# A placing model whose two DMA rings share the engines by packet size, and two kinds of work offered some microseconds later

## The chip, the cores and the metric

The kernel runs on one core of one Trainium2 chip. TensorE (PE in the profile) multiplies, ScalarE (ACT) evaluates functions and copies, VectorE (DVE) does element-wise work, GpSimd (POOL) and SyncE (SP) issue transfers here. The metric is device microseconds, the median of several executions; lower is better. The kernel before takes 735.46 us (three runs, 735.04 to 735.61).

## The reference, cut to what matters

```
x : 2048 x 640 (f32);  32 heads of 20
A: qkv = x @ wqkv;  pq, pk = phi(q), phi(k)      phi(t) = (t + 1 if t > 0 else exp(t)) + 1e-6
   kv = sum_s pk^T v;  z = sum_s pk
   o = (pq @ kv) / (pq . z + 1e-6)               per head and row
   a = o @ wo
B: h = sigmoid(x @ w_gate) * (x @ w_up)          640 -> 1536
   b = h @ w_down                                1536 -> 640
g = sigmoid(sum(x * gate_w))
result = g * a + (1 - g) * b
```

## The kernel before, in words

Every f32 matmul is done as three passes over values that are split into a high and a low half (`mm3`, lines 404 to 406). `split` (line 434) makes the halves: ScalarE writes the high half, VectorE then the low one. Sums of blocks of x, of weights and of hidden values save block products, so VectorE and ScalarE have a lot to add and split beside the matmuls.

The program has these stages:

- Stage 1 makes k from x and gathers x^T phi(k), from which kv follows later.
- Stage 2 (`q_phase` and `f_phase` with `pr` = 1) does the second 1024 rows of x. It makes q, the matrix M (kv times wo, for all heads together), and the twelve hidden blocks f = 0 to 11 of B. Each block's weights are loaded raw (`wst`), split and summed (`queue_g`, `queue_s`), and the finished halves and sums are stored in DRAM (`wf`). The pieces are called `wg`, `wu` and `ws`; a block's seven products `s1` to `s7` fill the PSUM tiles `ch`, `dd` and `cc`, and ScalarE copies some of them out into tiles `c` and `cx` before PE goes on adding in the same bank.
- Stage 3 does the same for the first 1024 rows. The finished weights are loaded from DRAM. After each second hidden block a pair of blocks goes through w_down (`down_pair`, line 1838); its weights are one tile `wf`, loaded in three parts by `load_wf` (line 1630): columns 640 to 1280 first, then 0 to 640, then the sums.
- Stage 4 multiplies the scaled phi(q) by M and finishes the output.

Two side works run in stage 3, beside the hidden blocks:

- Denominators (`queue_dens`, line 1399), for two groups of 512 rows at a time. POOL loads phi(q) tiles (`pden`), VectorE adds them up weighted into `fac`. The sums go to DRAM (`den_dram`) and come back turned (`turn_in`); `factor` adds the turned parts, takes the reciprocal and multiplies by the gate. The result is stored (`fac_dram`) and comes back turned once more (`turn_out`).
- M's rows (`queue_m`, line 1675), five row groups u = 0 to 4, one after the other in one tile. SP loads the rows in four transfers (`mr<-m_dram`), ScalarE and VectorE split them (`mt<-mr`), POOL stores the split rows (`mp_dram<-mt`), and the next group's load follows the split.

The order of the instructions on each engine is decided when the program is built, by the class `Order`. It keeps a clock for PE, ACT and DVE, with costs of `a_cost` and `v_cost`. Work is queued with a function that tells when its inputs are there (`ready`); `fill` gives an item its place when its inputs are there by these clocks and it ends soon enough behind PE (`_fits`). Transfers have a clock too: `Ring` stands for one of two queues, SP's and POOL's, and `Rings.issue` works out when a transfer lands if both queues have transfers under way. The builder's clocks set only the order; on the chip, engines wait for semaphores, in that order.

The lines that the change touches: `Rings.issue` (308), `Ring.dma_start` (352), `turn_in` (1420) and `queue_m` (1675). The result of `Rings.issue` is read by every `order.when(...)`, so that a changed landing time can move any queued work.

Of the kernel before, what the change touches and what calls it, by code (L numbers as in the profile page):

```python
# [15 lines left out]
S, D, F = 2048, 640, 1536  # L16
H, DH = 32, 20
KC = D // P
# [284 lines left out]
class Rings:  # L303
# [1 line left out]
    def __init__(self):  # L305
        self.q = [[], []]

    def issue(self, n, arrive, took):
        cell = [0.0]
        self.q[n].append((arrive, took, cell))  # L310
        i, t, left = [0, 0], 0.0, [None, None]
        q = self.q
        while True:
            for k in range(2):
                if left[k] is None and i[k] < len(q[k]) and q[k][i[k]][0] <= t:
                    left[k] = q[k][i[k]][1]
            live = [k for k in range(2) if left[k] is not None]
            coming = [q[k][i[k]][0] for k in range(2) if left[k] is None and i[k] < len(q[k])]
            if not live:
                if not coming:  # L320
                    break
                t = min(coming)
                continue
            dt = min([left[k] * len(live) for k in live] + [c - t for c in coming])
            t += dt
            for k in live:
                left[k] -= dt / len(live)
                if left[k] <= 1e-9:
                    q[k][i[k]][2][0] = t + 0.5
                    left[k] = None  # L330
                    i[k] += 1
        return cell


class Ring:

    def __init__(self, engine, order, rings, n, issue, lag):
        self.engine, self.order, self.rings, self.n, self.issue, self.lag = engine, order, rings, n, issue, lag
        self.t = 0.0
# [12 lines left out]
    def dma_start(self, out, src, **kw):  # L352
        o = self.order
        start = max(self.t, o.data(out, [src]))
        self.t = start + self.issue
        (r1, n), (r2, _) = (self.run(ap, 0 if getattr(ap.tensor, "_space", DRAM) == DRAM else 1) for ap in (out, src))
        r = min(r1, r2)
        took = 1.25 * max(1, n // r) * (7 + 0.0377 * r) / 16e3
        self.cell = self.rings.issue(self.n, start + self.lag, took)
        o.put(out, [src], self.cell)  # L360
        return self.engine.dma_start(out, src, **kw)

# [2 lines left out]
def a_cost(w):  # L365
    return 0.06 + w / 1200

def v_cost(w):
    return 0.07 + w / 960

@with_exitstack
def gated_mix_kernel(ctx: ExitStack, tc: tile.TileContext, xt, xn, wk, wv, wo, wst_q, wst_f, out_t):
# [6 lines left out]
    order = Order()  # L379
# [3 lines left out]
    def f32(ap):  # L383
        return ap.bitcast(F32)
# [34 lines left out]
    def vec2(out, a, b, op, after=""):  # L419
        order.on_vec(width(out), after, 1.0, out, a, b)  # L420
        nc.vector.tensor_tensor(out, a, b, op=op)  # L421

    def vec3(out, a, scalar, b, op0, op1, after=""):
        order.on_vec(width(out), after, 1.0, out, a, b)
        nc.vector.scalar_tensor_tensor(out, a, scalar, b, op0=op0, op1=op1)

    def vec1(out, a, s0, s1=None, op0=OP.mult, op1=None, after=""):
        order.on_vec(width(out), after, 1.0, out, a)
        if op1 is None:
            nc.vector.tensor_scalar(out, a, s0, None, op0=op0)  # L430
        else:
            nc.vector.tensor_scalar(out, a, s0, s1, op0=op0, op1=op1)

    def split(hi, lo, src, after=""):
        act(hi, src, AF.Copy, after)
        at = order.act + A_LAG

        def low():
            order.vec = max(order.vec, at)
            vec2(lo, src, f32(hi), OP.subtract)  # L440
        order.then(low)

    def add(out, a, b, after=""):
        vec2(out, a, b, OP.add, after)

    def sub(out, a, b, after=""):
        vec2(out, a, b, OP.subtract, after)
# [7 lines left out]
    fac = common.tile([P, NG, TG], F32, name="fac")  # L455
# [77 lines left out]
    class Chunk:  # L533
# [39 lines left out]
        def sum(self, n):  # L573
            x = self.x
            b11, b12, b21, b22 = x[0][:, 0:2], x[1][:, 0:2], x[0][:, 2:4], x[1][:, 2:4]
            self.T = (b11, b22, b12, b21)
            if n == 0:
                sub(b11, b12, b11)
            elif n == 1:
                sub(b12, b22, b12)  # L580
            elif n == 2:
                sub(b22, b22, b11)
            else:
                sub(b21, b21, b22)
# [434 lines left out]
    g = GTBatch(0, [0])  # L1019
# [8 lines left out]
    for c in range(1, 4):  # L1028
        ck = chunks[c]
        if c == 1:  # L1030
# [14 lines left out]
            g = GTBatch(c, batches[c])  # L1045
# [97 lines left out]
        if c > 1:  # L1143
            g = GTBatch(c, batches[c])
# [50 lines left out]
    def tt(name, dt=F32, shape=(P, TG)):  # L1195
        return pw.tile(list(shape), dt, name=name, tag="t", bufs=4)
# [202 lines left out]
    def queue_dens(*gs2):  # L1399

        st = {}

        def load(g, u):
            if u < KC:
                st[g, u] = tt("pden")
                gp.dma_start(st[g, u], p_dram[:, u, g])
                st["at", g, u] = lambda: order.when(st[g, u])

        def one(g, u):
            td = fac[:, g]  # L1410
            if u == 0:
                vec1(td, st[g, u], zcol[:, 0:1], zeps[:, 0:1], OP.mult, OP.add)
            else:
                vec3(td, st[g, u], zcol[:, u:u + 1], td, OP.mult, OP.add)
            load(g, u + 2)
            if u == KC - 1:
                gp.dma_start(den_dram[:, g], td)
                st["at", g, u + 1] = lambda: order.when(den_dram[:, g])

        def turn_in(g):  # L1420
            for j in range(4):
                js = slice(j * H, (j + 1) * H)
                gp.dma_start(fac[js, g].rearrange("h (d c) -> h d c", c=P),
                                  den_dram[:, g, j * P:(j + 1) * P].rearrange("(d h) c -> h d c", h=H))
            st[g, "gs"] = tt("gs")[:, :P]
            sp.dma_start(st[g, "gs"], gate_rep[4 * g:4 * g + 4].rearrange("i h c -> (i h) c"))
            st["at", g, KC + 1] = lambda: max(order.when(fac[:, g]), order.when(st[g, "gs"]))

        def factor(g):
            td = fac[:, g]  # L1430
            q = td[:, :P]
            add(td[:, :2 * P], td[:, :2 * P], td[:, 2 * P:])
            add(q, q, td[:, P:2 * P])
            order.on_vec(5 * P, "")
            nc.vector.reciprocal(q, q)
            vec2(q, q, st[g, "gs"], OP.mult)
            gp.dma_start(fac_dram[:, g], q)
            st["at", g, KC + 2] = lambda: order.when(fac_dram[:, g])

        def turn_out(g):  # L1440
            for d in range(4):
                sp.dma_start(fac[d * H:(d + 1) * H, g].rearrange("h (j c) -> h j c", c=P),
                                  fac_dram[:, g].rearrange("(j h) c -> h j c", h=H))
        order.add(0, 0, lambda: [load(g, u) for u in range(2) for g in gs2], chain=True)
        for u in range(KC):
            for g in gs2:
                order.add(0, v_cost(TG), lambda g=g, u=u: one(g, u), None, lambda g=g, u=u: st["at", g, u](), chain=True)
        for n, (v, fn) in enumerate(((0, turn_in), (2.0, factor), (0, turn_out))):
            for g in gs2:
                order.add(0, v, lambda g=g, fn=fn: fn(g), ("fac", g) if n == 2 else None,  # L1450
                          lambda g=g, n=n: st["at", g, KC + n](), chain=True)
# [217 lines left out]
    def m_rows(dst, cols, queue, u=None):  # L1669

        for d in range(4):
            m = m_dram.rearrange("(h u d) n -> d h u n", u=KC, d=4)[d]
            queue.dma_start(dst[d * H:(d + 1) * H], m[:, u] if cols is None else m[:, :, cols])

    def queue_m(u=0):

        raw = down_pool[1].tile([P, D], F32, name="mr", tag="mr")
        m_rows(raw, None, sp, u)

        def fn():  # L1680
            t = down_pool[1].tile([P, 2, D], F32R, name="mt", tag="mt")
            split(t[:, 0], t[:, 1], raw)

            def rest():
                gp.dma_start(mp_dram[:, u], f32(t))
                if u + 1 < KC:
                    queue_m(u + 1)
            order.then(rest)
        order.add(a_cost(D), v_cost(D), fn, "m", lambda: order.when(raw), spare=True)

    def m_close():
        nonlocal tb
# [510 lines left out]
    q = q_phase(1, lambda k: [(b12h[:, k], b12l[:, k])], extra)  # L2203
# [33 lines left out]
    q = q_phase(0, lambda k: [(c_h[c][:, k], c_l[c][:, k]) for c in range(2)], {})  # L2237
# [383 lines left out]
```

## Time and profile before

| | |
|---|---|
| median of 3 runs | 735.46 us (735.04 to 735.61) |
| the profiled execution | 735.37 us; its span 733.6 us |
| PE busy | 727.4 us, 99% of the span |
| DVE, ACT, POOL busy | 561.5, 358.6, 114.0 us |
| DMA | 173.54 MB, mean 237 GB/s |
| granted TensorE clock | 1.00 |

The profile lists, for one execution, the instructions of each engine with start and duration, what each waited for, and the transfers. Times within it count from the start of the span. `x4` at the end of a timeline row means four instructions merged in one row; the bracket names the idle time of the engine just before, and what ended it. In stage 3 the hidden blocks run from about 440 us on.

### The profile page before, as it was taken

The page shows a single profiled execution, that of the slowest core. Times are in us where ns is not written, and L with a number is a line of the kernel's source. Part 1 is how long each engine was busy: PE and PEld are TensorE (multiplying, and loading weights), DVE is VectorE, ACT ScalarE, POOL GpSimd, SP SyncE. Part 2 cuts the span into 40 slices and gives each one's busy share as a digit, 9 for nine tenths or more (in the row PEclk, how much of TensorE's full clock was granted, in tenths as well). Part 3 has the DMA queues.
Part 4 walks back from the last instruction along what each step waited for, and adds up shares of the span by engine and source line. Part 5 has one row for each costly group of instructions (what it writes and reads, how often), then busy time and mean ns, then how long its engine had stood idle before and what let it go on. Part 6 is the DMA issues. An engine that isn't in the chain of part 4 may idle for free.

```text
span 733.6 us, 10128 instructions
## 1 busy us (share of the span) xinstructions
PE 727.4 (99%) x3575; PEld 623.3 (85%) x3575; DVE 561.5 (77%) x987; ACT 358.6 (49%) x668; POOL 114.0 (16%) x197
## 2 busy tenths in 40 slices
PE   9999999999999999999999999999999999999998
PEld 8999999988788888888888888888787888888886
DVE  4978787987677989898989973466766775688783
ACT  5765648358556653535355363454333232324550
POOL 0211111113211211111210033023011331000000
PEclk9999999999999999999999999999999999999999
DMA  8464648697877866457687289878968597759212
GB/s 270 119 189 120 186 108 250 151 334 284 295 271 264 327 240 242 183 215 257 256 326 265 102 291 373 321 240 280 363 242 326 172 324 204 273 207 347 76 69 101
DMA packets 68873, 173.54 MB, mean 237 GB/s; under 512 B 11690, under 2 KB 31418, under 8 KB 65238
## 3 DMA queue, kind: packets, MB, share of 16 engines
q1 hardware_dynamic: 50342, 103.70, 42.7%
q0 software_dynamic: 18336, 69.03, 26.7%
q8 instruction: 28, 0.46, 0.3%
q14 instruction: 23, 0.19, 0.1%
q10 hardware_dynamic: 144, 0.16, 0.1%
HBM read 103.96 MB, written 63.92 MB: 229 GB/s over the span
## 4 chain that ended last, share of the span: by engine, by line
PE 86%; DMA 6%; issue 4%; DVE 2%; ACT 1%; POOL 1%; SPq 0%; POOLq 0%; ACTq 0%; DVEq 0%
PE ch L404 9%; PE ch L406 9%; PE ch L405 9%; PE cc L404 7%; PE cc L405 7%; PE cc L406 7%; PE dd L404 7%; PE dd L406 7%; PE dd L405 7%; PE rot L404 6%; PE rot L406 5%; PE rot L405 5%; DMA mr<-m_dram 2%; DMA pden<-p_dram 2%; DMA wg<-wf 1%
## 5 line engine op out<-in xcount | busy, mean ns | idle before, releaser
L417 ACT ACTIVATE c<-ch 128x512 f32<-128x512 f32 x52 | 31.1, 598 | 91.4 <-PE ch L406 91.3
L421 DVE TENSOR_TENSOR hf<-c,hf 128x512 fp32r<-128x512 f32 x75 | 51.2, 688 | 21.1 <-ACT hf L417 20.7
L417 ACT ACTIVATE hf<-c 128x512 fp32r<-128x512 f32 x75 | 46.1, 624 | 26.0 <-DVE c L421 26.0
L421 DVE TENSOR_TENSOR c<-cc,c 128x512 f32<-128x512 f32 x40 | 27.6, 689 | 40.6 <-PE cc L406 29.2
L404 PE MATMUL ch<-xth,ws 128*128 128x512 f32 x112 | 43.8, 391 | 0.0
L406 PE MATMUL ch<-xth,ws 128*128 128x512 f32 x112 | 43.6, 389 | 0.0
L405 PE MATMUL ch<-xtl,ws 128*128 128x512 f32 x112 | 43.6, 389 | 0.0
L421 DVE TENSOR_TENSOR tb<-rot,tb 128x512 f32<-128x512 f32 (+1 forms) x61 | 39.5, 677 | 3.0 <-PE rot L406 3.0
L421 DVE TENSOR_TENSOR tb<-dd,tb 128x512 f32<-128x512 f32 x44 | 30.3, 688 | 9.4 <-PE dd L406 9.4
L404 PE MATMUL dd<-xrh,wg 128*128 128x512 f32 x90 | 35.2, 391 | 0.0
L406 PE MATMUL dd<-xrh,wg 128*128 128x512 f32 x90 | 35.1, 389 | 0.0
L405 PE MATMUL dd<-xrl,wg 128*128 128x512 f32 x90 | 35.0, 389 | 0.0
L417 ACT ACTIVATE c<-dd 128x512 f32<-128x512 f32 x22 | 13.1, 598 | 41.4 <-PE dd L406 41.4
L404 PE MATMUL cc<-xbh,ws 128*128 128x512 f32 x84 | 32.7, 389 | 0.0
L405 PE MATMUL cc<-xbl,ws 128*128 128x512 f32 x84 | 32.7, 389 | 0.0
L406 PE MATMUL cc<-xbh,ws 128*128 128x512 f32 x84 | 32.7, 389 | 0.0
L421 DVE TENSOR_TENSOR c<-c,c 128x512 f32<-128x512 f32 x46 | 31.6, 688 | 1.3 <-ACT c L417 0.7
L417 ACT ACTIVATE dd<-ch 128x512 f32<-128x512 f32 x22 | 12.8, 582 | 35.0 <-PE ch L406 35.0
L421 DVE TENSOR_TENSOR wst<-wst 128x256 f32<-128x256 f32 (+2 forms) x69 | 27.4, 413 | 1.5
L404 PE MATMUL rot<-pkh,xnh 128*128 128x320 f32 x90 | 28.1, 312 | 0.1
L405 PE MATMUL rot<-pkl,xnh 128*128 128x320 f32 x90 | 27.8, 309 | 0.0
L406 PE MATMUL rot<-pkh,xnl 128*128 128x320 f32 x90 | 27.8, 309 | 0.0
(650 smaller groups left out, 2350.8 us busy)
## 6 DMA issues: line engine op xcount, KB each, us to landing
wf<-ws POOLq DMA_DIRECT2D x12, 1152.0 KB, 7.7
ws<-wf SPq DMA_DIRECT2D x11, 1152.0 KB, 9.5
wst<-wst_f SPq DMA_DIRECT2D x12, 640.0 KB, 5.2
wf<-wg POOLq DMA_DIRECT2D x12, 640.0 KB, 6.4
wd<-wd POOLq DMA_DIRECT2D x12, 640.0 KB, 8.0
wg<-wf SPq DMA_DIRECT2D x12, 640.0 KB, 5.8
wf<-wd SPq DMA_DIRECT2D x10, 640.0 KB, 10.1
xnst<-xn SPq DMA_DIRECT2D x16, 320.0 KB, 4.3
```

What stands on the lines that cost most here:

```text
L404: nc.tensor.matmul(out, l_hi, r_hi, start=first, stop=False, skip_group_check=True)
L405: nc.tensor.matmul(out, l_hi, r_lo, start=False, stop=False, skip_group_check=True)
L406: nc.tensor.matmul(out, l_lo, r_hi, start=False, stop=last, skip_group_check=True)
L417: nc.scalar.activation(out, src, fn, **kw)
L421: nc.vector.tensor_tensor(out, a, b, op=op)
```

## The change

In the builder's model, two transfers under way on both queues shared the 16 DMA engines half and half. Now each has a share in proportion to 7 + 0.0377 times its packet length in bytes, the length cut at 2600. And two kinds of work are offered later than the model's landing: the adding of the turned denominators by 4 us, the split of M's rows by 3 us. No instruction computes anything else than before.

```diff
-    def issue(self, n, arrive, took):
+    def issue(self, n, arrive, took, share):
         cell = [0.0]
-        self.q[n].append((arrive, took, cell))
+        self.q[n].append((arrive, took, cell, share))
...
-            dt = min([left[k] * len(live) for k in live] + [c - t for c in coming])
+            all_ = sum(q[k][i[k]][3] for k in live)
+            part = {k: q[k][i[k]][3] / all_ for k in live}
+            dt = min([left[k] / part[k] for k in live] + [c - t for c in coming])
             t += dt
             for k in live:
-                left[k] -= dt / len(live)
+                left[k] -= dt * part[k]
...
-        self.cell = self.rings.issue(self.n, start + self.lag, took)
+        self.cell = self.rings.issue(self.n, start + self.lag, took, 7 + 0.0377 * min(r, 2600))
...
-            st["at", g, KC + 1] = lambda: max(order.when(fac[:, g]), order.when(st[g, "gs"]))
+            st["at", g, KC + 1] = lambda: max(order.when(fac[:, g]), order.when(st[g, "gs"])) + 4
...
-        order.add(a_cost(D), v_cost(D), fn, "m", lambda: order.when(raw), spare=True)
+        order.add(a_cost(D), v_cost(D), fn, "m", lambda: order.when(raw) + 3, spare=True)
```

What this does to the built program, engine by engine (the two orders laid side by side):

- PE has the same matmuls in the same order.
- ACT and DVE differ at three places. At two places in stage 2, raw weights are split later: one split of 640 columns (`wg<-wst`) goes behind a copy `c<-ch`; and in hidden block f = 0 the split `wg` of the next block's weights goes from ahead of the loading of a function table to behind the copy `c<-ch` that follows it. The sums of that block's weights (`wst<-wst`) and its split `ws` come later with it: on ACT the copy `cx<-ch` now stands ahead of the split `ws`, and on DVE the addition `cx<-cc,cx` stands between the second and the third of the five sums.
- At the third place, in stage 3, the five splits of M's rows each move back by some instructions, and the factors of the first two groups of denominators, side by side before, are now apart: the first behind the split of row group 2, the second behind the split `hf` of the next hidden block.
- SP issues the rows of groups 2 and 3 later: before, groups 0, 1 and 2, then `gs`, `wu`, `wg`, `ws`, three parts of `wf`, group 3, `wu`; now groups 0 and 1, `gs`, `wu`, group 2, `wg`, `ws`, three parts of `wf`, `wu`, group 3. Group 4 stays behind `fac<-fac_dram`.
- POOL stores row group 0 behind `den_dram<-fac` instead of ahead of it, and group 1 behind `fac<-den_dram` instead of ahead of it. The stores of groups 2 to 4 keep their places, and `pden<-p_dram` of the next two groups stays behind the store of group 4.

## The prediction

> **What bounds the kernel now.** First the page, for the engines' shares:
>
> ```profile
> span 733.6 us, 10128 instructions
> PE 727.4 (99%) x3575; PEld 623.3 (85%) x3575; DVE 561.5 (77%) x987; ACT 358.6 (49%) x668; POOL 114.0 (16%) x197
> ```
>
> PE is the bound, and its matmuls stay the same. So the change can only win what PE waits, and lose by new waits. Second the waits of PE alone (columns: who waits, for whom, us, times, longest):
>
> ```profile
> PE rot L404 <- DVE tb L421: 0.9, 1, 0.9
> ...
> PE ch L404 <- ACT cx L417: 0.4, 1, 0.4
> PE dd L404 <- DMA wf<-wd: 0.2, 1, 0.2
> ```
>
> The lines left out are the wait at the start and one of 0.2 us on ACT `ms`, ahead of which no order changes. These three lie at or behind a place where it does. What each costs, the timeline of PE tells (start, duration, instruction):
>
> ```profile
> 194.68 0.39 PE L406 MATMUL ch<-xth,ws 128*128 128x512 f32 x1
> 194.91 0.39 PE L404 MATMUL ch<-xah,wg 128*128 128x512 f32 x1
> ...
> 196.04 0.39 PE L406 MATMUL ch<-xah,wg 128*128 128x512 f32 x1
> 196.83 0.50 PE L404 MATMUL ch<-xth,wu 128*128 128x512 f32 x1 [0.40 <-ACT cx L417]
> ...
> 518.87 0.39 PE L406 MATMUL ch<-xth,ws 128*128 128x512 f32 x1
> 519.49 0.50 PE L404 MATMUL dd<-hf,wf 128*128 128x512 f32 x1 [0.23 <-DMA wf<-wd]
> ...
> 567.82 0.39 PE L406 MATMUL cc<-hf,wf 128*128 128x512 f32 x1
> 569.14 0.47 PE L404 MATMUL rot<-hf,wf 128*128 128x512 f32 x1 [0.94 <-DVE tb L421]
> ```
>
> Matmuls of 512 columns start 0.23 apart (194.68 to 194.91). Across the three waits the starts are 0.79, 0.62 and 1.32 apart, and the first matmul behind each is 0.11, 0.11 and 0.08 longer than 0.39. So they cost 0.56 + 0.11 = 0.67, 0.39 + 0.11 = 0.50 and 1.09 + 0.08 = 1.17 us: 2.34 us together, 0.32% of the time. That is all that the change can plausibly win.
>
> **The change, part by part.** *The raw weights of stage 2.* Third view: the timelines of ACT and DVE around the first wait, with the next use of these weights on PE.
>
> ```profile
> 166.56 0.73 ACT L417 ACTIVATE wg<-wst 128x640 fp32r<-128x640 f32 x1
> ...
> 189.80 0.73 ACT L417 ACTIVATE wg<-wst 128x640 fp32r<-128x640 f32 x1
> 195.55 0.74 ACT L417 ACTIVATE ws<-wst 128x640 fp32r<-128x640 f32 x1 [2.18 <-DVE wst L421]
> 196.20 0.58 ACT L417 ACTIVATE cx<-ch 128x512 f32<-128x512 f32 x1
> ...
> 193.51 2.01 DVE L421 TENSOR_TENSOR wst<-wst 128x256 f32<-128x256 f32 x5
> ...
> 203.08 0.39 PE L404 MATMUL ch<-xth,ws 128*128 128x512 f32 x1
> ```
>
> Before, the split `ws` at 195.55 waited 2.18 us for the five sums on DVE, and the copy `cx<-ch`, whose bank PE wants back, stood behind it. PE had finished that bank at 194.68 + 0.39 = 195.1. In the new order `cx` stands ahead of `ws`. It can start then and ends 0.58 later, at 195.7; PE asks for the bank at 196.04 + 0.23 = 196.27. The wait goes, all 0.67. What is late next is `ws`: the addition `cx<-cc,cx` on DVE takes its place among the sums, and the last three of them (three fifths of 2.01, 1.2) end near 197.6. The splits of both halves of `ws` follow on ACT and DVE, by estimate some 3 us (0.74 for one on ACT, as much again for each other piece), to about 200.5. PE uses `ws` at 203.08 − 0.67 = 202.4. The cover is 1.9 us; without it each us would count in full. `wg`, moved from 189.80 behind the copy (by estimate to 192.3, its low half done by 193.9), is first used at 194.91. Bounds: a gain of 0.67, a loss of 0 for the rest; I take −0.67.
>
> The other moved `wg` (166.56) goes behind one copy, and can push what follows on ACT by its own 0.73. No wait of PE lies within 10 us behind it. Between 0 and 0.73, taken as 0.
>
> *Row groups 0 to 2, and the wait for `wf`.* Fourth view: the timeline of SP, the splits on ACT (ns, first and last start), the timeline of POOL, the store's size (and us to landing), and the stretch ahead of the wait (columns of the last row: us, busy time of PE, PEld, DVE, ACT and POOL, clock, DMA share, GB/s).
>
> ```profile
> 499.82 1.78 SPq L361 DMA_DIRECT2D mr<-m_dram  x4
> 506.05 1.83 SPq L361 DMA_DIRECT2D wf<-wd  x3
> 507.98 4.38 SPq L361 DMA_DIRECT2D mr<-m_dram  x4
> ...
> L417 ACT ACTIVATE mt<-mr x5: 732/740/741, 490.5 to 536.8; 128x640 fp32r<-128x640 f32 x5
> ...
> 507.47 0.56 POOL L361 DMA_DIRECT2D mp_dram<-mt  x1 [2.45 <-DVE mt L421]
> ...
> mp_dram<-mt POOLq DMA_DIRECT2D x5, 640.0 KB, 4.8
> ...
> 512.00:519.00 7.00, 7.00 (x33) 5.66 (x31) 6.76 (x14) 1.53 (x3) 0.56 (x1) 1.00 1.01 402
> ```
>
> The DMA engines are full (1.01, 402 GB/s), so `wf` lands when the bytes ahead of it are through. The splits move: group 0 behind four copies into `tb`, from 490.5 to about 494.7; by the same reading of the new order group 1 to about 502, group 2 to about 513, with its low half on DVE at 515. SP's rows of group 2 are issued at about 503.8 instead of 499.82, still ahead of `wf`, so the same four transfers are ahead of it in both orders, and `wf` itself is still issued near 506. On POOL the store of group 2 (640 KB) leaves the stretch: 507.47 becomes about 515.8. The store of group 1 stays in it, now behind `fac<-den_dram`. So up to 640 KB fewer go ahead of `wf`: 1.6 us at 402 GB/s. Against it stands that the engines idle longer near 495, as group 0's store and group 1's rows start some 3 us later; about 1 us of it may be missing later. `wf` then lands between 1.6 us earlier and 1.1 us later than before; 0.50 suffices. I take −0.50, with +1.1 as the other end.
>
> *The factors of the denominators.*
>
> ```profile
> 514.90 0.74 DVE L421 TENSOR_TENSOR fac<-fac 128x256 f32<-128x256 f32 x2
> ```
>
> They did not wait for their transfer before (no bracket), so 4 us of delay buy nothing there. The second goes behind `hf`, to about 521, and pushes an addition into `tb` by an estimated 0.5. The stored result is fetched behind `wf`, as before. 0, with a cover of some us.
>
> *Row groups 3 and 4, and the wait at 569.* Fifth view: DVE and POOL, then the queues' shares (queue: packets, MB, share of the engines) in 539 to 542, 560 to 562, and 562 to 564.
>
> ```profile
> 537.57 0.82 DVE L421 TENSOR_TENSOR mt<-mr,mt 128x640 fp32r<-128x640 f32 x1 [0.64 <-ACT mt L417]
> 540.29 0.69 DVE L421 TENSOR_TENSOR hf<-c,hf 128x512 fp32r<-128x512 f32 x1
> ...
> 563.38 0.75 DVE L425 SCALAR_TENSOR_TENSOR fac<-pden,zcol,fac 128x512 f32<-128x512 f32 x1 [2.38 <-DMA pden<-p_dram]
> 568.31 1.28 DVE L421 TENSOR_TENSOR tb<-rot,tb 128x512 f32<-128x512 f32 x2
> ...
> 538.69 0.54 POOL L361 DMA_DIRECT2D mp_dram<-mt  x1 [9.81 <-DVE mt L421]
> 539.22 2.15 POOL L361 DMA_DIRECT2D pden<-p_dram  x4
> 556.72 1.06 POOL L361 DMA_DIRECT2D pden<-p_dram  x2 [15.35 <-DVE fac L432]
> ...
> 536.00:539.00 3.00, 3.00 (x15) 2.46 (x14) 2.36 (x5) 0.74 (x1) 0.31 (x1) 1.00 0.01 4
> ...
> q0 software_dynamic: 94, 0.48, 42.9%
> q1 hardware_dynamic: 81, 0.25, 29.4%
> ...
> q1 hardware_dynamic: 71, 0.59, 71.5%
> q0 software_dynamic: 60, 0.23, 28.2%
> ...
> q0 software_dynamic: 211, 0.69, 90.2%
> ```
>
> PE waits at 569 for the addition at 568.31, which stands on DVE behind the one at 563.38, and that waited 2.38 us for `pden`. In the new order the last split of M's rows goes behind `hf` (540.29), so it ends near 541.0 instead of 538.4. The store and the four `pden` behind it on POOL move by some 2.4 us. Ahead of 539 the engines were idle (share 0.01), and POOL's queue q0 moved 0.48 MB in 539 to 542. Now SP's queue is there alone, and moves perhaps 0.40 MB in place of 0.48 + 0.25 = 0.73. So 0.33 MB are missing, 0.8 us at some 400 GB/s, and from there until 562 SP's queue is never empty. The two `pden` issued at 556.72 got little while SP's queue had work (0.23 MB beside 0.59 in 560 to 562) and most after (0.69 MB in 562 to 564). I take that they land 0.8 us later, and DVE hands that on to PE. A gain is excluded here, since nothing on either queue gets earlier behind 539; the other end is the whole shift, 2.4. Taken: +0.8, the row of missing bytes.
>
> [...]
>
> **Sum.** −0.67 − 0.50 + 0.80 = −0.37. The profiled execution took 735.37 (span 733.6 and 1.8 around it), so 735.0; the median of the runs, 735.46, lies 0.09 above it, so 735.1.
>
> **The rivals.** *The third wait does not grow.* The missing bytes find a gap before 556. For it: the 0.40 MB is an estimate, and SP's queue may fill more of the stretch. Against it: q0 got only what q1 left. 735.46 − 1.17 = 734.3.
>
> *All three waits go.* The row groups' loads, away from the front, let `pden` in before SP's queue fills. Against it: it is issued at 556.72 only when DVE frees its tile, and PE sets that. 735.46 − 2.34 = 733.1.
>
> *Slower: group 2's rows hold up `wf`.* They are issued between `wu` and `wg` at 503.8, and if they keep the queue as long as their delay less the 1.5 us by which `wu` gets ahead, `wf` is 3.9 − 1.5 = 2.4 late. It decides once `wf` is over 0.4 late. At half of that, 1.2: −0.67 + 1.2 + 0.8 gives 736.8; at all of it 738.0. For it: full engines in 512 to 519. Against it: the same bytes stood ahead before. One more idle stretch of PE would then be near 3 us. [...]
>
> *The change does not do what it says: transfers, not PE, set stage 3.* Then `wf` lands when it did, PE comes 0.67 earlier and waits 0.67 longer. That gives 735.5, and 736.3 if the third wait grows. For it: the engines are full from 506 on. Against it: each of these transfers is issued when PE frees a tile.
>
> **How the numbers follow.** Chances: forecast 0.38, third wait unchanged 0.22, transfers set it 0.16, slower by `wf` 0.14, all waits gone 0.10. A measurement of this kernel can tell about 0.2%, 1.47 us: 733.99 and 736.93 are the bounds. Faster: the 0.10, and 0.06 from the lower edge of the second case, 0.16. Slower: half of the `wf` case and 0.05 of the forecast's and the fourth case's upper edges, 0.12. Same: 0.72. The range runs from 733.6, between all and two waits gone, to 736.8, the middle of the `wf` case; outside lie about 0.09 below and 0.10 above. The forecast's own range is 734.3 to 736.0.
>
> **What would show it.** Step 1: no wait of PE on ACT `cx` near 196. Step 2: no wait on `wf<-wd` near 518. Step 3: POOL's last store of split rows 2 to 3 us later relative to PE, `pden` landing later, the wait on `tb` longer than 1. The waits of ACT for `mr<-m_dram` should shrink, and bring nothing. Wrong it would be by a new PE wait in stage 2, or one on `wf`'s second part.

## The result, and the profile after

The changed kernel takes 733.52 us (median of 14 runs, 733.11 to 734.58); the kernel before 735.22 (14 runs, 733.62 to 736.06, among them the three that gave 735.46). The ratio from all these runs is 0.9982, with a 95% interval of 0.9974 to 0.9989 (the two medians alone would give 0.9977, inside it); a second measurement (experiment 9) gave 0.9985 (0.9976 to 0.9994). That is 1.1 to 1.3 us faster: real, and still within the 0.2% that the prediction called no change. The forecast's own sum, -0.37 us or a ratio of 0.9995, lies outside both intervals. The rival "the third wait does not grow", -1.17 us or 0.9984, lies in both.

The page, and below it the waits of PE (who waits, for whom, us, times, longest):

```profile
span 732.0 us, 10131 instructions
...
PE 726.3 (99%) x3575; PEld 623.4 (85%) x3575; DVE 561.2 (77%) x987; ACT 358.6 (49%) x668; POOL 114.3 (16%) x197
```

```profile
PE rot L406 <- DVE tb L423: 1.0, 1, 1.0
...
PE dd L406 <- ACT ms L419: 0.2, 1, 0.2
```

Of the three waits, those on ACT `cx` and on DMA `wf` are gone and the one on DVE `tb` is left. The timeline of PE at the three places:

```profile
195.50 0.39 PE L408 MATMUL ch<-xah,wg 128*128 128x512 f32 x1
195.73 0.39 PE L406 MATMUL ch<-xth,wu 128*128 128x512 f32 x1
...
517.66 0.39 PE L408 MATMUL ch<-xth,ws 128*128 128x512 f32 x1
517.89 0.39 PE L406 MATMUL dd<-hf,wf 128*128 128x512 f32 x1
...
565.32 0.39 PE L408 MATMUL dd<-hf,wf 128*128 128x512 f32 x1
565.60 0.50 PE L406 MATMUL cc<-hf,wf 128*128 128x512 f32 x1
...
566.16 0.40 PE L408 MATMUL cc<-hf,wf 128*128 128x512 f32 x1
567.55 0.47 PE L406 MATMUL rot<-hf,wf 128*128 128x512 f32 x1 [0.99 <-DVE tb L423]
```

At the first two places the starts are 0.23 apart, which is no wait. At the third they are 1.39 apart, a cost of 1.16 + 0.08 = 1.24 us where it was 1.17; a small one of 0.05 + 0.11 stands just ahead of it. From the last `dd<-hf,wf` ahead of both to the second `rot<-hf,wf` behind them PE takes 2.53 us, where it took 2.34: the place as a whole costs 0.19 more.

The span fell by 1.6 us. Of that, 0.35 was there before any changed instruction ran: the first matmul of stage 2, in the timelines of the kernel before and of the changed one,

```profile
144.86 0.39 PE L404 MATMUL dd<-xrh,wg 128*128 128x512 f32 x1
```

```profile
144.51 0.39 PE L406 MATMUL dd<-xrh,wg 128*128 128x512 f32 x1
```

starts 0.35 earlier, with the same code up to there. From this matmul to the end of the span it is 588.74 us before and 587.49 after: 1.25 us less, which is the number to compare with the ratio.

The other engines at these places:

```profile
194.56 0.60 ACT L419 ACTIVATE cx<-ch 128x512 f32<-128x512 f32 x1 [1.75 <-PE ch L408]
...
196.91 1.26 ACT L419 ACTIVATE ws<-wst 128x640 fp32r<-128x640 f32 x2 [0.39 <-DVE wst L423]
...
199.03 0.68 DVE L423 TENSOR_TENSOR ws<-wst,ws 128x512 fp32r<-128x512 f32 x1
...
201.85 0.39 PE L406 MATMUL ch<-xth,ws 128*128 128x512 f32 x1
...
503.13 1.80 SPq L363 DMA_DIRECT2D mr<-m_dram  x4
...
506.58 2.00 SPq L363 DMA_DIRECT2D wf<-wd  x3
...
514.81 0.56 POOL L363 DMA_DIRECT2D mp_dram<-mt  x1 [10.86 <-DVE mt L423]
...
539.98 2.15 POOL L363 DMA_DIRECT2D pden<-p_dram  x4
554.89 1.06 POOL L363 DMA_DIRECT2D pden<-p_dram  x2 [12.76 <-DVE fac L434]
...
561.79 0.75 DVE L427 SCALAR_TENSOR_TENSOR fac<-pden,zcol,fac 128x512 f32<-128x512 f32 x1 [2.62 <-DMA pden<-p_dram]
```

`cx` starts when PE has finished the bank and ends at 195.16, 0.57 ahead of PE. `ws` is done at 199.71, 2.1 ahead of its use. The store of row group 2 is issued at 514.81 in place of 507.47. The four `pden` come at 539.98 in place of 539.22, and as PE is 1.8 us earlier by then (the `dd<-hf,wf` at 565.32 stood at 567.11), that is 2.6 later for PE. DVE's wait for `pden` is 2.62 us in place of 2.38.

### The profile page after: what moved, and what is told of

It is laid out like the page before. It is cut to its first block, busy times and chain, and to the rows that moved or that the text cites. A ratio compares the mean times of both kernels' runs of the same rounds, so it can differ in the third digit from the quotient of the medians.

```text
span 732.0 us, 10131 instructions
## 1 busy us (share of the span) xinstructions
PE 726.3 (99%) x3575; PEld 623.4 (85%) x3575; DVE 561.2 (77%) x987; ACT 358.6 (49%) x668; POOL 114.3 (16%) x197
## 4 chain that ended last, share of the span: by engine, by line
PE 96%; issue 2%; DVE 1%; POOL 1%; DMA 0%; ACT 0%; POOLq 0%; DVEq 0%
PE ch L406 10%; PE ch L407 10%; PE ch L408 10%; PE cc L407 8%; PE cc L406 8%; PE cc L408 8%; PE dd L406 7%; PE dd L407 7%; PE dd L408 7%; PE rot L406 6%; PE rot L407 6%; PE rot L408 6%; PE rot L494 0%; DVE tb L423 0%; DMA m_dram<-ms 0%
```

## The experiments

The costs of the waits in this table are read from the timeline of PE in the prediction's way: start to start, less 0.23, plus what the matmul behind the wait is longer than 0.39. "Stage 2 to end" is the span less the start of `dd<-xrh,wg`. The fourth place, near 497, is a wait of PE in `rot<-hf,wf` that neither of the first two profiles has.

| kernel | ratio to before (95%) | at 196 | at 497 | at 518 | at 566 | stage 2 to end, us |
|---|---|---|---|---|---|---|
| before | | 0.67 | 0 | 0.50 | 1.17 | 588.74 |
| changed | 0.9982 (0.9974 to 0.9989) | 0 | 0 | 0 | 1.24 | 587.49 |
| 1 stage 2 alone | 0.9992 (0.9983 to 1.0001) | 0 | 0.39 | 0.48 | 1.22 | 588.38 |
| 2 stage 3 alone | 0.9999 (0.9991 to 1.0008) | 0.60 | 0.40 | 0 | 1.24 | 588.54 |
| 3 row groups 0 to 2 alone | 0.9998 (0.9986 to 1.0010) | 0.65 | 0.35 | 0 | 1.22 | 588.71 |
| 4 last row group alone | 1.0003 (0.9995 to 1.0012) | 0.67 | 0.21 | 0.47 | 1.22 | 589.17 |
| 5 `ws` in four loads | 0.9974 (0.9964 to 0.9984) | 0 | 0 | 0 | 0.67 | 586.56 |
| 6 `ws` in two loads | 0.9975 (0.9966 to 0.9984) | 0 | 0 | 0 | 0.54 | 586.61 |
| 7 sums of u = 2 later | 0.9970 (0.9958 to 0.9981) | 0 | 0.40 | 0 | 0 | 586.53 |
| 8 and sums of u = 4 later | 0.9967 (0.9954 to 0.9979) | 0 | 0 | 0 | 0 | 586.04 |
| 9 changed, again | 0.9985 (0.9976 to 0.9994) | 0 | 0 | 0 | 1.24 | 587.53 |

The intervals of 1 to 4 are wider than the effects, and those of 5 to 8 overlap the changed kernel's, so the verdict is the trace's, place by place, from one profile of each. Not in the table are the small waits just ahead of 566: from the last `dd<-hf,wf` to the second `rot<-hf,wf` there, PE takes 2.34 us before, 2.53 and 2.50 in the two profiles of the changed kernel, 2.49 in 1 and in 3, 2.58 in 2 and 2.59 in 4.

**1. Stage 2 alone.** The new shares hold until stage 3 is planned, equal ones after; no +4, no +3.

```diff
-        self.q = [[], []]
+        self.q, self.uneven = [[], []], True
...
-... 7 + 0.0377 * min(r, 2600))
+... 7 + 0.0377 * min(r, 2600) if self.rings.uneven else 1.0)
...
+        if not pr:
+            rings.uneven = False
```

> The kernel before with the new shares in stages 1 and 2 alone: stage 3 is planned as before, so only the two places of raw weights in stage 2 differ. Theory (PE's waits set the time): the wait of PE on ACT `cx` near 196 goes (0.56 + 0.11 us), the waits on `wf` near 518 and on `tb` near 568 stay with 0.50 and 1.17; -0.67 us against the kernel before, ratio 0.9991. Rival (transfers set stage 3): the 0.67 us come back as a longer wait on `wf<-wd`, some 1.2 in place of 0.50; 0 against the kernel before.

Measured: 0.9992. The waits of PE, and its timeline near 497:

```profile
PE rot L406 <- DVE tb L423: 1.0, 1, 1.0
...
PE dd L406 <- DMA wf<-wd: 0.2, 1, 0.2
```

```profile
496.01 0.39 PE L408 MATMUL dd<-hf,wf 128*128 128x512 f32 x1
496.51 0.50 PE L406 MATMUL rot<-hf,wf 128*128 128x512 f32 x1
```

The wait on `cx` is gone, the one on `wf` is 0.48, not 1.2: the 0.67 us don't come back there. So the transfers of stage 3 follow PE, and the rival falls. The second fence is the fourth place: starts 0.50 apart, too short a gap for the list of waits. It eats 0.28 + 0.11 = 0.39 of the gain in this execution. Experiments 2 and 3 have it too, with the wait on `cx` still there, so it is not the 0.67 us coming back in another place.

**2. Stage 3 alone.** Equal shares everywhere, with the +4 and the +3; on all engines, stage 3 then has the changed kernel's order and stage 2 that of before.

```diff
-            all_ = sum(q[k][i[k]][3] for k in live)
-            part = {k: q[k][i[k]][3] / all_ for k in live}
+            all_ = sum(1 for k in live)
+            part = {k: 1 / all_ for k in live}
```

> The other part alone: equal shares everywhere, with the +4 and the +3, so that stage 2 is as before and stage 3 has the order of the changed kernel. Theory: the wait on `cx` stays (0.67), the one on `wf` goes (-0.50), the one on `tb` is as in the changed kernel (+0.1 to +0.2): -0.3 to -0.4 us, ratio 0.9995. By the prediction's third step as it stood, +0.8 instead of +0.2: +0.3 us. Rival (the wait on `wf` went only because PE came 0.67 us earlier out of stage 2 and the transfers with it): the wait stays and the sum is +0.2.

Measured: 0.9999. The wait on `wf` goes here too, with PE as late as before, so that one is the work of stage 3's order and not of an earlier PE. The wait on `tb` is 1.24, as in the changed kernel, and the fourth place costs 0.40. It follows that the new shares act in stage 2 only, and the two offsets in stage 3 only.

**3. Row groups 0 to 2 alone.** The kernel before, with one edit:

```diff
-        order.add(..., lambda: order.when(raw), spare=True)
+        order.add(..., lambda: order.when(raw) + 3 * (u < 3), spare=True)
```

> The kernel before with the +3 for row groups 0, 1 and 2 alone; the last two groups, the sums of denominators and stage 2 stay in their places. Theory (moving the stores and rows of groups 0 to 2 away from the stretch ahead of `wf` is what lets it land in time): the wait on `wf` goes, -0.50, the one on `tb` stays at 1.17 within 0.2; ratio 0.9993. Rival (it is the sums of denominators moved behind `hf` on DVE, or the late groups): the wait on `wf` stays, 0.

Measured: 0.9998. Of the three places, PE's waits still have

```profile
PE rot L404 <- DVE tb L421: 1.0, 1, 1.0
...
PE ch L404 <- ACT cx L417: 0.4, 1, 0.4
```

No line on `wf` is left. The built order moves more than the expectation says: the first factors of the denominators come 10 us sooner (504.37 in place of 514.90), and the split of the last row group goes behind `hf`, as in the changed kernel, so that the four `pden` are issued at 540.73. But the second factors stand ahead of `hf` here, and the rows of the last two groups stand behind `wf` on SP's queue in both orders, so neither part of the rival is needed. The queues (packets, MB, share of the engines) in 509 to 518, in the kernel before and in this one:

```profile
q1 hardware_dynamic: 667, 2.55, 79.0%
q0 software_dynamic: 205, 0.77, 22.8%
```

```profile
q1 hardware_dynamic: 926, 3.50, 98.8%
q0 software_dynamic: 32, 0.07, 2.0%
```

POOL's 0.77 MB, most of it the store of group 2 (640 KB), are gone from this stretch, and SP's queue, with `wf` in it, moves 0.95 MB more; in the changed kernel it is 3.58 MB, and nothing on POOL's. The rows of group 2 stand ahead of `wf` on SP's queue in both orders. So it is most likely the store, but no run moves it without the rows.

**4. The last row group alone.** The kernel before, with `+ 3 * (u == 4)` in the same line.

> The kernel before with the +3 for the last row group alone: on ACT its split stands behind one `hf`, on DVE behind three additions, and its store and the four `pden` behind it on POOL come some 2.4 us later. By the prediction's third step: `pden` lands 0.8 us later, the wait on `tb` is 2.0 in place of 1.17, +0.8 us, ratio 1.0011. Theory from the trace of the changed kernel (`pden` takes its turns beside SP's queue and does not wait until that has run dry): SP's queue is some 2.5 us further behind near 560, `pden` lands 0.1 to 0.3 later, and the wait and the time grow by as much; ratio 1.0003.

Measured: 1.0003. This is the prediction's third step by itself. PE at the third place, and then the landing of the `ws` issued ahead of `pden` and of the `pden` itself (KB, us from issue to landing):

```profile
567.93 0.40 PE L406 MATMUL cc<-hf,wf 128*128 128x512 f32 x1
569.30 0.47 PE L404 MATMUL rot<-hf,wf 128*128 128x512 f32 x1 [0.97 <-DVE tb L421]
```

```profile
ws<-wf SPq DMA_DIRECT2D x1, 1152.0 KB, 12.0
...
pden<-p_dram POOLq DMA_DIRECT2D x1, 256.0 KB, 6.8
```

The changed kernel shows the same two lines. In the kernel before they are:

```profile
ws<-wf SPq DMA_DIRECT2D x1, 1152.0 KB, 9.5
...
pden<-p_dram POOLq DMA_DIRECT2D x1, 256.0 KB, 6.6
```

SP's queue is 2.5 us further behind, and all of that falls on SP's own `ws`; `pden` lands 0.2 later and PE's wait grows by 0.05, the place as a whole by 0.25 (2.59 us for 2.34). Of this 0.25, experiment 1, whose stage 3 is in the order of before, shows 0.15 too, so that at most some 0.1 is clear of what executions differ by. The +0.8 of the third step is refuted.

**5 and 6. Smaller loads on SP's queue.** The changed kernel with the one `ws` load that runs beside `pden` cut into four (5) or two (6).

```diff
-        for c0, c1 in (...) if n == ("f", 0, 0) and i == 2 else ((0, w),):
+        for c0, c1 in (...) if n in (("f", 0, 0), ("f", 0, 8)) and i == 2 else ((0, w),):          # 5
+        ... else ((0, 4 * P), (4 * P, w)) if n == ("f", 0, 8) and i == 2 else ((0, w),):           # 6
```

> The changed kernel with the one `ws` load that runs beside `pden` near 560 cut into four of 256, 256, 256 and 384 columns: the same bytes, in rows of 1,024 to 1,536 bytes in place of 9,216. Theory (the two queues take turns by packets, so `pden` gets its share beside SP's queue, and the share follows SP's packet size): in 558 to 562 POOL's queue moves over 0.25 MB per us in place of some 0.12, the `pden` issued near 554.9 lands 1 to 2 us sooner (near 560 in place of 561.70), DVE waits 0.5 to 1.5 in place of 2.62, and PE's wait on `tb` near 566 shrinks from 1.24 to under 0.3: some 1 us faster than the changed kernel, ratio to the kernel before 0.997, unless `ws`, now later, makes PE wait itself. Rival (shares of one half by bytes, or `pden` waits for its own start and not for SP's queue): `pden` lands at 561.7 as before, the wait stays 1.2, ratio 0.998.

> The same with two loads of 512 and 640 columns, rows of 2,048 and 2,560 bytes. Theory of turns by packets: a smaller effect of the same sign, POOL's queue near 0.2 MB per us in 559 to 561, `pden` lands 0.7 to 1.5 us sooner than 561.70, PE's wait on `tb` 0.2 to 0.7; ratio to the kernel before 0.9975. Rival: no change against the changed kernel, wait 1.2, ratio 0.998.

Measured: 0.9974 and 0.9975. First the changed kernel's queues (packets, MB, share of the engines) in 555 to 557.9, 558 to 560 and 560 to 562, then those of 5 in 558 to 560, then `pden`'s landing in 5 and in 6:

```profile
q1 hardware_dynamic: 331, 1.18, 102.7%
...
q1 hardware_dynamic: 108, 0.67, 82.1%
q0 software_dynamic: 42, 0.17, 21.3%
...
q1 hardware_dynamic: 68, 0.59, 72.0%
q0 software_dynamic: 73, 0.23, 29.2%
```

```profile
q0 software_dynamic: 131, 0.48, 63.4%
q1 hardware_dynamic: 251, 0.29, 41.8%
```

```profile
pden<-p_dram POOLq DMA_DIRECT2D x1, 256.0 KB, 6.1
```

```profile
pden<-p_dram POOLq DMA_DIRECT2D x1, 256.0 KB, 5.9
```

In 558 to 560 POOL's queue moves 0.48 MB in place of 0.17. Part of that is the window, in which its first packet comes 0.3 us sooner; over 1.66 us from its first packet on it is 0.47 MB in place of 0.22, with the same bytes on SP's queue in smaller rows. `pden` lands 0.7 and 0.9 us sooner behind its issue, and PE's wait falls from 1.24 to 0.67 and 0.54. So POOL's share of the bytes was larger beside smaller rows of SP's: 0.22 of 0.70 MB in 558.68 to 560.34 of the changed kernel, 0.48 of 0.77 in 558 to 560 of 5 and 0.41 of 0.78 in 6, and the rival of half shares falls. The size was missed: rows of 1,024 to 1,536 bytes did no better than rows of 2,048 and 2,560, and the wait did not go under 0.3. The first lines show the rest of it: issued at 554.89, `pden` has no packet on POOL's queue in 555 to 557.9, and the first one comes near 558.7. In 5 and 6, too, the first packet comes 3.8 us behind the issue (issued at 554.52, nothing on POOL's queue in 555 to 558), so the smaller rows left this part of the 6.8 us as it was. What sets it was not tested.

**7. The sums of the third `pden` later.** The changed kernel, for the two groups whose sums are queued at hidden block 7:

```diff
-                st["at", g, u] = lambda: order.when(st[g, u])
+                st["at", g, u] = lambda: order.when(st[g, u]) + 2 * (u == 2 and g < 2)
```

> The changed kernel with the sums of the third `pden` (u = 2) placed 2 us later on DVE for two groups: the addition that waited 2.62 us for `pden` stands behind two `hf` and one `tb<-cc`, and the second group's factors behind the two `tb<-rot`. Theory (PE's third wait is DVE's queue behind that addition): the wait on `tb` near 566 goes, 1.24 + 0.1 to 0.2 us off the changed kernel, ratio to the kernel before 0.9965. Rival (a chain of DVE work that is late anyway, or the factors later than PE can bear): PE waits as long at the next `rot` or at the end for the factors; ratio 0.998 or above.

Measured: 0.9970. No line on `tb` is left among PE's waits; near 497 its timeline and that of DVE show

```profile
496.71 0.39 PE L408 MATMUL rot<-hf,wf 128*128 128x512 f32 x1
497.23 0.50 PE L406 MATMUL rot<-hf,wf 128*128 128x512 f32 x1
...
493.82 1.42 DVE L427 SCALAR_TENSOR_TENSOR fac<-pden,zcol,fac 128x512 f32<-128x512 f32 x2 [0.65 <-DMA pden<-p_dram]
...
496.49 0.68 DVE L423 TENSOR_TENSOR tb<-rot,tb 128x512 f32<-128x512 f32 x1
```

The wait at 566 was DVE's queue behind an addition whose `pden` had not landed; with two `hf` and one `tb<-cc` ahead of it, nothing waits there. The factors that come later cost nothing. The fourth place is of the same kind: sums that waited for `pden`, and behind them the addition (it ends at 497.17) that gives PE its bank back.

**8. Both places.** Kernel 7 with `+ 2 * (u == 4 and g > 1)` added to the same line, which puts one `tb<-rot` on DVE ahead of the last sum near 494, and the second ahead of the split `mt`.

> The kernel of the later sums (u = 2, two groups) with the last sum (u = 4) of the other two groups placed 2 us later as well, which puts one `tb<-rot` on DVE ahead of the last of those sums, near 495. Theory (the wait of PE near 497, 0.0 to 0.4 in the profiles so far, comes from DVE's queue behind `pden` whose landing differs between executions): that wait is gone and the one near 566 too, PE waits for nothing from 200 to 570 longer than 0.1; ratio to the kernel before 0.9967, 0 to 0.4 us under the kernel of the later sums. Rival (the sums are late anyway and push PE's next bank): a wait of 0.3 or more on `tb` stays within 495 to 500; ratio 0.997.

Measured: 731.90 us, 0.9967, the fastest here. What is left of PE's waits, and DVE near 494:

```profile
PE rot L494 <- PEq L2614: 0.8, 1, 0.8
PE dd L406 <- ACT ms L419: 0.2, 1, 0.2
```

```profile
493.31 0.69 DVE L423 TENSOR_TENSOR tb<-rot,tb 128x512 f32<-128x512 f32 x1
493.91 0.74 DVE L427 SCALAR_TENSOR_TENSOR fac<-pden,zcol,fac 128x512 f32<-128x512 f32 x1
494.57 0.68 DVE L423 TENSOR_TENSOR tb<-rot,tb 128x512 f32<-128x512 f32 x1
```

From stage 2 to the end it is 586.04 us, 2.70 less than before; the three waits of the prediction were 2.34. Its interval and that of 7 overlap, and one profile without the wait near 497 does not prove it gone, as others lack it too.

**9. The changed kernel again.**

> The changed kernel once more. Theory: the wait near 566 is 1.24 again, no wait near 196 and 518, ratio 0.998; the start of stage 2 (147.50 in its first profile, 146.99 to 147.86 in the others, all with the same code up to there) and the wait near 497 (0 in its first profile, up to 0.4 in others) differ by some tenths between executions. Rival (these belong to the changed order): both come out as in its first profile.

Measured: 0.9985. The waits at the three places are as in its first profile, to 0.01 us. Stage 2 begins at 143.97 in place of 144.51 (the expectation counts from a matmul 3.0 us further on), so that start differs by 0.54 us between two executions of one kernel; over all eleven profiles it is 143.97 to 144.86. The wait near 497 is 0 in both profiles of this kernel.

## Why the prediction was right or wrong

- **PE is the bound, and only its three waits can be won: right.** From stage 2 to the end, less the sum of its four places, every kernel takes 585.9 to 586.6 us, and kernel 8, with no wait there, is 2.70 us under the kernel before. That is 0.36 more than the three waits; 0.15 of it is a small wait on ACT `c` near 190, which the profile of the kernel before has and those of 2 and 3, with the same order there, have not.
- **Raw weights of stage 2, -0.67: right.** `cx` moved ahead of `ws`, experiment 1 takes the wait away by itself, and the cover of `ws` was 2.1 us where 1.9 was worked out. The other `wg`, taken as 0, cost PE nothing.
- **Row groups 0 to 2, -0.50: right.** Rows of group 2 at 503.13 (worked out: 503.8), its store at 514.81 (515.8), `wf` still issued near 506; the wait is gone, and experiments 2 and 3 put it down to the order of these groups, as worked out: POOL's store is out of the stretch ahead of `wf`. The slow case, with `wf` over 0.4 late, did not come.
- **Factors, 0: right.** DVE still adds them without waiting, and PE has no wait near them.
- **Row groups 3 and 4, +0.80: wrong.** The shift was right: the four `pden` came 2.6 us later for PE (worked out: 2.4), and SP's queue fell 2.5 us behind. The step that failed is the next one, that `pden` "got little while SP's queue had work" and so would land as much later as bytes were missing. No run shows the +0.80: the wait measured +0.05 by itself (experiment 4) and +0.07 in the changed kernel; with the small wait ahead of it the place costs 0.25 and 0.19 more, and 0.15 more where stage 3 is unchanged (experiment 1). The backlog fell on `ws`, which nobody was waiting for. The rows quoted could have said it: in 560 to 562, while SP's queue moved 0.59 MB, POOL's moved 0.23, and the one `pden` that PE depends on has only 0.26. So most of it had gone through beside SP's queue, and little could gain from that queue's running dry. The landings agree: `ws`, issued at 555.27, landed 9.5 us later at 564.8, and this `pden`, issued at 556.72, 6.6 us later at 563.3, ahead of it. Most of the 0.69 MB of 562 to 564 belonged to later `pden`.
- **POOL's queue beside SP's: more than the "little" of the third step.** In the changed kernel POOL's queue moved 0.17 MB in 42 packets in 558 to 560, which is 4.0 KB each, beside SP's 8.7 KB in 560 to 562 (0.59 MB in 68). One packet of each in turn would give POOL 4.0 / 12.7 = 32%, an estimate from these two; measured in 560 to 562 it is 0.23 / 0.82 = 28%. Counted from POOL's first packet on, the packets are near equal: 60 of SP's queue beside 55 in the changed kernel (558.68 to 560.34), and 157 beside 130 in experiment 5 (558.34 to 560). In 560 to 562 of experiment 5 they are 478 beside 79, so near equality is shown for these first stretches alone.
- **The forecast against the rivals.** What came is the first rival's number, with a chance of 0.22, but not its mechanism: there was no gap in which the bytes were made up, as SP's queue stayed 2.5 us behind; beside that longer queue `pden` landed 6.8 us behind its issue, where it was 6.6. That the time stayed within the 0.2% called no change says nothing for the third step, since the two gains without it (1.17 us) stay within it as well. The result's 733.52 us lies 0.8 below that rival's 734.3 and just under the range's edge of 733.6. The trace tells of that: 0.35 us of the profiled pair is the start, which differs between executions; the rest, 588.74 to 587.49, is 1.25 us, against that rival's 1.17. The agreement is in part chance: the third place cost 0.19 more, and the small wait near 190 of the kernel before, 0.15, was not in the forecast.
- **ACT's waits for M's rows: right.** They were 11.3 us in four waits before and are now

```profile
ACT mt L419 <- DMA mr<-m_dram: 1.2, 1, 1.2
```

and nothing of these 10 us reached PE.

What stays open: the wait near 497 came in five of eleven profiles, 0.21 to 0.40 us. It is 0 in both profiles of the changed kernel and in 5 and 6, which have its order there, but 0.40 in 2 and 7, which have it too. Whether the changed order makes it rarer can't be said from so few. It may be why the ratios of experiments 1 and 2 together, 0.9992 x 0.9999 = 0.9991, stay short of 0.9982; their intervals are wide enough to cover that by themselves.

## What to carry to other kernels

When an engine waits for a transfer on one queue, first ask how much of its bytes have moved by the time the other queue runs dry. In the kernel before `pden` landed at 563.3, ahead of the `ws` beside it at 564.8, and 2.5 us more on SP's queue made `pden` land only 0.2 us later (experiment 4). Smaller rows on SP's queue brought it 0.7 and 0.9 us sooner behind its issue (5 and 6), and of its 6.8 us 3.8 passed before its own first packet. The late transfer cost PE what stood behind its addition on DVE (a wait of 2.62 us there, 1.24 on PE), so moving that addition behind work that is ready (experiments 7 and 8) won more at its place here (all of the 1.24 us) than making the transfer faster (0.57 and 0.70 in 5 and 6). And with effects of half a microsecond in 735, measure each place in the trace from a common point behind the noisy start (0.9 us between the earliest and the latest of eleven profiles); the ratio of medians does not tell one cause from another.

## What the runs showed of the hardware

- With the engines full (share 1.04 in 555 to 558.6), a `pden` load of the changed kernel, issued on POOL at 554.89, moved its first packet near 558.7, 3.8 us later. With the engines idle (share 0.01 in 538.7 to 539.8 of the kernel before), a store issued on POOL at 538.69 moved its first packet 1.1 us later.
- Cutting a 1,152 KB load on SP's queue into smaller rows, bytes unchanged, raised the other queue from 0.22 (changed kernel) to 0.47 MB (experiment 5) in 1.66 us from its first packet on; 2 KB rows did as well for the landing (5.9 us) as 1 to 1.5 KB rows (6.1 us), and 9 KB rows gave 6.8.
- The same instructions reach stage 2 anywhere from 143.97 to 144.86 us, a spread of 0.9 us, larger than two of the three effects studied (0.67, 0.50 and 1.17).
